# The convolution half of a two-layer kernel, rewritten as 337 pieces in one fixed order, with the transposes and the short convolution on TensorE

## The chip, the cores and the metric

One core of one Trainium2 chip. The metric is the device time of one execution in microseconds (us); smaller is better. Runs of the kernel before scatter over 1%. Engines are named as the profile names them: PE is TensorE (PEld its weight loads), DVE is VectorE, ACT is ScalarE, POOL is GpSimd, SP issues the loads and stores.

## The reference, cut to what matters

Two layers, each made of a gated long convolution (`_A_ref`) and an MLP (`_B_ref`), over 2048 tokens of 512 channels. The convolution of the first layer and that of the second have the same `k`, `v` and filter, so both kernels compute its result `y` once (in `YA`) and use it twice.

```python
def _A_ref(q, k, v, shift_k, ssm_k, ssm_D):
    # k_shift: 4-tap causal convolution of k along the tokens, per channel
    for t in range(ks):
        k_shift = k_shift + k_pad[:, t:t + S, :] * shift_k[:, ks - 1 - t][None, None, :]
    kv = k_shift * v
    # y: kv convolved with ssm_k over the whole length 2048 (by FFT of 4096), per channel
    y_f = rfft(kv padded) * rfft(ssm_k padded)
    y = irfft(y_f)[:S] + kv * ssm_D
    return q * y

def _B_ref(x, w1, b1, w2, b2):            # 512 -> 1376 -> 512
    h = gelu(layernorm(x) @ w1 + b1)
    return h @ w2 + b2

x = q
for layer in range(2):
    x = x + _A_ref(layernorm(x), k, v, shift_k, ssm_k, ssm_D)
    x = x + _B_ref(layernorm(x), w1, b1, w2, b2)
```

Both kernels do the long convolution as a transform in two stages, by matrix products with tables. A "first stage" multiplies by `Ft` over 128 partitions, a transposition brings the other index into the partitions, and a "second stage" multiplies by one table of `Wt` for each of 32 frequencies. The spectrum of `kv` (called X) is multiplied by that of the filter (called K, in `ZK`, with its swapped halves in `KSW`). The inverse goes back the same way: tables `Mt` (called V), a transposition, tables `Gt` (called Y).

## The kernel before

The short convolution and the product with `v` are on VectorE, 28 + 4 operations of 128x2048 elements on four blocks of 128 channels:

```python
    def kv_chunk(cc):                                                   # line 148
        ...
        nc.vector.tensor_tensor(m[:], kh[:, h:h + NT, c0:c0 + CW], sb(0), ALU.mult)
        for t in range(1, KS):
            m2 = rot.tile([P, NT, CW], BF16, name="kvt", tag="kvt")
            nc.vector.tensor_tensor(m2[:], kh[:, h - t:h - t + NT, c0:c0 + CW], sb(t), ALU.mult)
            nc.vector.tensor_tensor(m[:], m[:], m2[:], ALU.add)
        nc.vector.tensor_tensor(uv[:, :, c0:c0 + CW], m[:], uv[:, :, c0:c0 + CW], ALU.mult)
```

The first stage ends in a transposition on VectorE, eight times (K and `kv`, four blocks each), and so does the inverse, four times:

```python
        def stage1(src, dst, cc, tag):                                  # line 191
            ...
            for q in range(4):
                pz = ps.tile([P, 8, CW], F32, name="pz", tag=tag)
                for i in range(8):
                    tau = 8 * (q % 2) + i
                    nc.tensor.matmul(pz[:, i, :], Ft[:, q // 2, :], src[:, tau, c0:c0 + CW], start=True, stop=True)
                nc.scalar.activation(ZT[:, 8 * q:8 * q + 8, :], pz[:], AF.Copy)
            nc.vector.transpose(dst[:, :, c0:c0 + CW].bitcast(F32).rearrange("p k c -> p c k"),
                                ZT[:].bitcast(F32).rearrange("p b c -> p c b"))
        ...
        k_transpose()                                                   # line 209
        for cc in range(NCH):
            kv_chunk(cc)
            stage1(Ktok, ZK, cc, "pa")
            stage1(uv, ZX, cc, "pb")
        ...
        for j in range(NA // 2):                                        # second stage of K
            k_stage2(j)
        ...
        for j in range(NA // 2):                                        # X, product T, inverse V
            T = x_mul(j)
            if pend is not None:
                x_inv(j - 1, pend)
            pend = T
        ...
        for cc in range(NCH):                                           # line 264
            c0 = cc * CW
            nc.vector.transpose(V2[:, :, c0:c0 + CW].bitcast(F32).rearrange("p k c -> p c k"),
                                ZX[:, :, c0:c0 + CW].bitcast(F32).rearrange("p b c -> p c b"))
        for t2 in range(NT // 2):                                       # output Y
            ...
```

The second stage works on whole rows of 512 channels, so each loop over j needs every block of the loop ahead of it: all first stages before any second stage, all inverses before any inverse transposition. After that come the gate, a layernorm and the MLP: eight groups (two layers of four) of 512 tokens. `prep` (two layernorms and a gate on VectorE) of the next group is issued beside the MLP of this one.

## Time and profile before

| | before |
|---|---|
| time, median of 4 runs | 340.26 us (338.0 to 340.95) |
| span and granted clock of the profiled run | 337.7 us, 0.884 |
| busy PE / DVE / ACT | 243.3 / 225.2 / 164.5 us |
| first MLP matmul | 170.13 us |

The busy numbers hide what matters: 72%, 67% and 49% of the span are averages over stages with different limits. So the page's slices, its chain, and the table by stage are to be read together. Two words to know for them: the "front" is all up to the first MLP matmul, and the granted clock is the share of full speed that TensorE was allowed.

### The profile page before, as it was taken

How to read it: one execution, taken by the hardware profiler on the slowest of the kernel's cores; microseconds unless marked ns; L12 is line 12 of the kernel's file. 1: busy time of each engine (PE TensorE's matmuls, PEld its weight loads, DVE VectorE, ACT ScalarE, POOL GpSimd, SP SyncE). 2: the span in 40 equal slices, each digit the busy share in tenths (PEclk: the TensorE clock that was granted, in tenths of full speed). 3: DMA queues.
4: the chain of work that ended last, by engine and by line, in shares of the span. 5: the costliest groups of instructions: out<-in, count | busy, mean ns of one | idle time of the engine just before them, and what ended most of it. 6: DMA issues, size and time to landing. Idle time of an engine off the chain costs nothing.

```text
span 337.7 us, 3467 instructions
## 1 busy us (share of the span) xinstructions
PE 243.3 (72%) x1292; PEld 123.1 (36%) x1312; DVE 225.2 (67%) x361; ACT 164.5 (49%) x206; POOL 19.8 (6%) x26
## 2 busy tenths in 40 slices
PE   0007646253675987007599999989999999999995
PEld 0007646152321332002235444444444444444442
DVE  2208999999543999894887987888787682020122
ACT  0106877055779887004667736246271643826300
POOL 3000000000010000001102112101011110000000
PEclk9999767556587999656969999999999999999999
DMA  7990000006589444000000000000000001010011
GB/s 235 369 390 4 2 0 2 0 0 249 188 227 225 108 167 167 0 0 0 2 0 1 2 0 0 2 0 1 3 0 0 2 0 52 12 46 17 18 62 47
DMA packets 7040, 21.94 MB, mean 65 GB/s; under 512 B 912, under 2 KB 4593, under 8 KB 5872
## 3 DMA queue, kind: packets, MB, share of 16 engines
q1 hardware_dynamic: 5890, 19.14, 17.9%
q10 hardware_dynamic: 1022, 2.59, 2.1%
q8 instruction: 10, 0.16, 0.2%
q0 software_dynamic: 112, 0.00, 0.1%
q14 instruction: 6, 0.05, 0.0%
HBM read 15.44 MB, written 2.10 MB: 52 GB/s over the span
## 4 chain that ended last, share of the span: by engine, by line
DVE 46%; PE 36%; DMA 8%; ACT 5%; POOL 3%; issue 2%; another core or an unknown queue 0%; DVEq 0%; POOLq 0%; ACTq 0%
PE po L328 17%; PE ph L316 14%; DVE arena L200 7%; DVE st L169 6%; DMA arena<-in_A_ssm_k_dram 6%; DVE arena L266 5%; DVE kvm L159 4%; DVE kvt L158 4%; DVE arena L177 4%; ACT arena L207 3%; DVE T L235 3%; POOL rs L173 3%; DVE arena L244 3%; DVE T L234 2%; DMA arena<-in_A_k_dram 2%
## 5 line engine op out<-in xcount | busy, mean ns | idle before, releaser
L328 PE MATMUL po<-arena 128*128 128x512 bf16 (+1 forms) x339 | 79.6, 379 | 2.1 <-DVE arena L331 1.4
L316 PE MATMUL ph<-arena 128*128 128x512 bf16 (+1 forms) x349 | 79.3, 386 | 0.8 <-ACT arena L308 0.7
L318 ACT ACTIVATE arena<-ph,B 128x512 bf16<-128x512 f32 (+1 forms) x88 | 60.2, 687 | 29.4 <-PE ph L316 27.4
L331 DVE TENSOR_TENSOR arena<-po,arena 128x512 bf16<-128x512 f32 x32 | 21.8, 682 | 50.1 <-PE po L328 50.1
L316 PEld LDWEIGHTS <-arena 128*128 128x128 bf16 (+1 forms) x352 | 35.8, 102 | 43.3 <-issue 3.8
L328 PEld LDWEIGHTS <-arena 128*128 128x128 bf16 (+1 forms) x352 | 33.8, 98 | 38.9 <-issue 1.5
L198 PE MATMUL pz<-arena,Ft 128*128 128x128 bf16 x256 | 26.7, 283 | 26.4 <-DVE arena L160 17.2
L169 DVE BATCH_NORM_STATS2 st<-arena 128x6 f32<-128x512 bf16 x64 | 42.4, 676 | 4.8 <-DMA arena<-in_A_q_dram 4.1
L199 ACT ACTIVATE ZT<-pz 128x1024 bf16<-128x1024 f32 x32 | 30.7, 1031 | 22.2 <-PE pz L198 21.9
L308 ACT ACTIVATE arena<-pt 128x512 bf16<-128x512 bf16 x32 | 17.3, 594 | 42.9 <-PE pt L307 42.7
L198 PEld LDWEIGHTS <-Ft 128*128 128x128 bf16 x256 | 23.7, 132 | 29.5 <-issue 25.0
L200 DVE STREAM_TRANSPOSE arena<-ZT 128x2048 f32<-128x2048 f32 x8 | 29.4, 3676 | 3.0 <-ACT ZT L199 3.0
L173 POOL TENSOR_TENSOR rs<-rs,mhalf 128x4 f32<-128x4 f32 x16 | 16.1, 1009 | 202.4 <-DVE rs L172 202.4
L187 PE MATMUL pk<-IDt,arena 128*128 128x128 bf16 x64 | 6.3, 279 | 27.2 <-DVE arena L143 26.6
L273 PE MATMUL py<-arena,Gt 128*128 128x512 bf16 x31 | 9.5, 450 | 18.1 <-DVE arena L266 17.6
L177 DVE TENSOR_SCALAR arena<-arena,rs,nm 128x512 bf16<-128x512 bf16 x64 | 22.1, 407 | 0.6
L242 PE MATMUL pv<-T,arena 128*128 128x512 bf16 x63 | 18.3, 388 | 3.3 <-DVE T L234 1.5
L274 ACT ACTIVATE arena<-py 128x1024 bf16<-128x1024 f32 x8 | 8.2, 1023 | 21.7 <-PE py L273 21.5
L232 ACT ACTIVATE xb<-px 128x1024 bf16<-128x1024 f32 x16 | 16.3, 1040 | 3.4 <-DVE T L235 3.3
L207 ACT ACTIVATE arena<-pk 128x1024 bf16<-128x1024 f32 x16 | 15.1, 1058 | 2.6 <-PE pk L206 2.6
L189 ACT ACTIVATE arena<-pk 128x2048 bf16<-128x2048 bf16 x4 | 7.2, 1883 | 18.7 <-PE pk L187 18.7
L266 DVE STREAM_TRANSPOSE arena<-arena 128x2048 f32<-128x2048 f32 x4 | 16.2, 4149 | 0.1
(38 smaller groups left out, 188.2 us busy)
## 6 DMA issues: line engine op xcount, KB each, us to landing
arena<-arena SPq DMA_DIRECT2D x8, 512.0 KB, 7.4
arena<-in_A_k_dram SPq DMA_DIRECT2D x1, 2048.0 KB, 12.6
arena<-in_A_ssm_k_dram ACTq DMA_DIRECT2D x4, 512.0 KB, 19.4
arena<-in_A_v_dram SPq DMA_DIRECT2D x1, 2048.0 KB, 12.7
arena<-tabM SPq DMA_DIRECT2D x1, 2048.0 KB, 7.6
arena<-in_A_q_dram SPq DMA_DIRECT2D x1, 2048.0 KB, 8.7
out_dram<-arena SPq DMA_DIRECT2D x16, 128.0 KB, 1.7
arena<-in_B_w_dram SPq DMA_DIRECT2D x1, 1376.0 KB, 5.9
```

Source lines behind the costliest of these rows:

```text
L169: nc.vector.bn_stats(st[:, i, :], x_t[:, GT * g + i, :])
L173: nc.gpsimd.tensor_tensor(rs[:], rs[:], mhalf[:], ALU.pow)
L177: nc.vector.tensor_scalar(out=dst[:, i, :], in0=x_t[:, GT * g + i, :], scalar1=rs[:, i:i + 1], scalar2=nm[:, i:i + 1], op0=ALU.mult, op1=A ...
L198: nc.tensor.matmul(pz[:, i, :], Ft[:, q // 2, :], src[:, tau, c0:c0 + CW], start=True, stop=True)
L199: nc.scalar.activation(ZT[:, 8 * q:8 * q + 8, :], pz[:], AF.Copy)
L200: nc.vector.transpose(dst[:, :, c0:c0 + CW].bitcast(F32).rearrange("p k c -> p c k"), ZT[:].bitcast(F32).rearrange("p b c -> p c b"))
L207: nc.scalar.activation(ZK[:, 2 * j:2 * j + 2, :], pk[:], AF.Copy)
L266: nc.vector.transpose(V2[:, :, c0:c0 + CW].bitcast(F32).rearrange("p k c -> p c k"), ZX[:, :, c0:c0 + CW].bitcast(F32).rearrange("p b c -> ...
L316: nc.tensor.matmul(ph[0:m, :], W1t[:, ct, ft * P:ft * P + m], lt[:, ct, :], start=ct == 0, stop=ct == CT - 1)
L318: nc.scalar.activation(ht[0:m, ft, :], ph[0:m, :], AF.Gelu_apprx_tanh, bias=B1[0:m, ft:ft + 1])
L328: nc.tensor.matmul(po[:], ht[0:m, ft, i * P:(i + 1) * P], W2t[0:m, ft, :], start=ft == 0, stop=ft == FT - 1)
L331: nc.vector.tensor_tensor(xs, po[:], xs, ALU.add)
```

## The change

The intent: take from VectorE what TensorE can do (the transpositions by a matmul against the identity, the short convolution by matmuls against diagonal matrices), cut every stage but K's second to blocks of 128 channels so that blocks need not wait for each other, and fix in which order each engine does the pieces, so that loads, TensorE-heavy and VectorE-heavy stages lie beside each other. Four PSUM slots of 1024 fp32 serve all pieces of the front. The order is a string.

```diff
+ORDER = """
+lK2.S lK1.S lK3.S lH.S lv0.S lK0.S lk2.S lW.S lv1.S lG.S lk0.S lk3.S lk1.S KT2.P0 KT2e.D dt2.D K2S0.P10 KT1.P2 K2S0e.A
...
+U2S3.P2 U2S0e.A U2S2.P0 U2S1.P1 U2S2e.A U2S3e.D U1T0.P3 U2S1e.A kv30.P0 U1T0e.D X10.P20 kvm30.D X11.P11 X10e.A U1T1.P3
+X11e.A U3S0.P00 T10.D0 U1T1e.D U0T0.P2 U3S0e.A U3S2.P1 U0T0e.D X13.P32 U3S2e.A U3S1.P0 U3S3.P2 T11.D1 X13e.A U0T1.P1
...
+"""
```

A word is a piece, its engine's letter (P, D, A, G for GpSimd, S) and the slots it takes. K2S0 is the first quarter of the first stage of K's block 2, K2S0e its copy out of PSUM, kv30 a part of the convolution and kvm30 its product with `v`, U the first stage of `kv`, T after a block the transposes. X10, T10, V10 are X, product and inverse of block 1, quarter 0; TP and Y the inverse's transposes and the output. The pieces are written down with

```diff
+    def write(self, order):
+        pieces = {it["name"]: it for it in self.items}
+        for word in order.split():
+            name, how = word.split(".")
+            it = pieces.pop(name)
+            it["eng"] = how[0]
+            it["slot"] = {ring: int(c) for ring, c in zip(it["take"], how[1:])}
+            it["fn"](it)
...
+        with tc.manual_schedule(engines={ENG.PE, ENG.Activation, ENG.DVE, ENG.Pool, ENG.SP}):
+            plan.write(ORDER)
+            n2 = prep(2)
```

and the work itself moves like this (cut):

```diff
-        nc.vector.tensor_tensor(m[:], kh[:, h:h + NT, c0:c0 + CW], sb(0), ALU.mult)
-        for t in range(1, KS): ...
+                    for i in range(8):                                          # kv
+                        for t in range(KS):
+                            tau = 8 * o2 + i - t
+                            w = kT[:, cc, tau, 2:2 + P] if tau >= 0 else kT[:, cc, tau + NT, 1:1 + P]
+                            nc.tensor.matmul(o[:, i, :], w, DG[:, cc, t, :], start=t == 0, stop=t == KS - 1)
...
-            nc.vector.transpose(dst[:, :, c0:c0 + CW].bitcast(F32).rearrange("p k c -> p c k"),
-                                ZT[:].bitcast(F32).rearrange("p b c -> p c b"))
+                    for i in range(16):                                         # T of a first stage
+                        zk = apf(ZTb[z["slot"]["zt"]], 16 * h + i, [[8 * D, P], [32, P]])
+                        nc.tensor.transpose(o[:, i, :], zk, IDt[:])
...
-            nc.vector.transpose(V2[:, :, c0:c0 + CW].bitcast(F32).rearrange("p k c -> p c k"),
-                                ZX[:, :, c0:c0 + CW].bitcast(F32).rearrange("p b c -> p c b"))
+                        for i in range(2 * m):                                  # TP
+                            vk = apf(ZTb[v0["slot"]["zt"]], 16 * (i // m) + t0 + i % m, [[8 * D, P], [32, P]])
+                            nc.tensor.transpose(o[:, i // m, i % m, :], vk, IDt[:])
...
-    with tc.tile_pool(name="ps2", bufs=3, space=bass.MemoryType.PSUM) as ps2, \
-            tc.tile_pool(name="ps3", bufs=2, space=bass.MemoryType.PSUM) as ps3:
+    with tc.tile_pool(name="ps2", bufs=3, space=bass.MemoryType.PSUM, reuse_waits="tile") as ps2, \
+            tc.tile_pool(name="ps3", bufs=2, space=bass.MemoryType.PSUM, reuse_waits="tile") as ps3:
```

The preps of the MLP's first three groups move into the ordered part (those of groups 0 and 1 cut into pieces, with some on ScalarE and GpSimd). The loops of the MLP stay as they were.

## The prediction

> **What bounds the kernel now.** I read the busy digits of the page first, then its chain of work, then a table of engine busy time by stage, then the groups of instructions by shape, then single stretches of the timeline for the pitch of back-to-back work.
>
> The busy digits (40 slices of 8.44 us, tenths):
> ```profile
> PE   0007646253675987007599999989999999999995
> ...
> DVE  2208999999543999894887987888787682020122
> ACT  0106877055779887004667736246271643826300
> ...
> PEclk9999767556587999656969999999999999999999
> ```
> PE is at 8 or 9 from the twenty-second slice to the last but one (the MLP). Before that, no engine is at 9 throughout: DVE is, then ACT, then DVE, in turn, and PE runs at a half-granted clock in between. The chain of work says the same:
> ```profile
> DVE 46%; PE 36%; DMA 8%; ACT 5%; POOL 3%; issue 2%; another core or an unknown queue 0%; DVEq 0%; POOLq 0%; ACTq 0%
> ```
> By stage (start:end, length, then busy us and counts of PE, PEld, DVE, ACT, POOL; granted clock; DMA):
> ```profile
> 0.00:26.60 26.60, 0.00 (x0) 0.00 (x0) 4.66 (x8) 1.28 (x1) 2.69 (x8) 1.00 0.87 317
> 26.60:92.30 65.70, 36.30 (x327) 30.60 (x329) 62.61 (x38) 41.31 (x40) 0.00 (x0) 0.67 0.15 53
> 92.30:107.10 14.80, 9.50 (x28) 3.10 (x28) 4.55 (x15) 12.42 (x15) 1.04 (x1) 0.85 0.94 238
> 107.10:137.50 30.40, 24.94 (x90) 8.29 (x92) 28.58 (x41) 22.60 (x23) 0.00 (x0) 0.95 0.50 141
> 137.50:153.70 16.20, 0.00 (x0) 0.00 (x0) 16.19 (x4) 0.00 (x0) 0.00 (x0) 0.50 0.00 0
> 153.70:170.10 16.40, 11.34 (x47) 4.83 (x48) 9.97 (x27) 10.36 (x13) 3.00 (x4) 0.81 0.00 1
> 170.10:337.70 167.60, 161.22 (x800) 76.27 (x815) 98.62 (x232) 76.57 (x117) 13.08 (x13) 0.99 0.04 13
> ```
> So there are two kernels in one. The front (170.1 us, up to the first MLP matmul) is a row of stages, each bound by another thing: 26.6 us of loads, 65.7 us of VectorE, 14.8 us of ScalarE, 30.4 us of VectorE, 16.2 us of VectorE alone, 16.4 us of a latency chain. The MLP (167.6 us) is TensorE at full clock: 704 matmuls of 512 columns at a pitch of 0.216 us are 152 us, the rest is transposes and ends. The change touches only the front in substance.
>
> The operations at stake (busy us, mean ns):
> ```profile
> L200 DVE STREAM_TRANSPOSE arena<-ZT 128x2048 f32<-128x2048 f32 x8 | 29.4, 3676 | 3.0 <-ACT ZT L199 3.0
> L266 DVE STREAM_TRANSPOSE arena<-arena 128x2048 f32<-128x2048 f32 x4 | 16.2, 4149 | 0.1
> L159 DVE TENSOR_TENSOR kvm<-kvm,kvt 128x2048 bf16<-128x2048 bf16 x12 | 14.4, 1210 | 0.1
> L158 DVE TENSOR_TENSOR kvt<-arena,SK 128x2048 bf16<-128x2048 bf16 x12 | 14.2, 1215 | 0.0
> L199 ACT ACTIVATE ZT<-pz 128x1024 bf16<-128x1024 f32 x32 | 30.7, 1031 | 22.2 <-PE pz L198 21.9
> L189 ACT ACTIVATE arena<-pk 128x2048 bf16<-128x2048 bf16 x4 | 7.2, 1883 | 18.7 <-PE pk L187 18.7
> ```
> and two timeline lines for the pitch:
> ```profile
> 43.05 0.61 PE L198 MATMUL pz<-arena,Ft 128*128 128x128 bf16 x8 [0.31 <-ACT ZT L199]
> 95.95 10.19 ACT L207 ACTIVATE arena<-pk 128x1024 bf16<-128x1024 f32 x11 [0.68 <-PE pk L206]
> ```
> Eight 128-column matmuls take 0.61 us, one alone 0.22: pitch (0.61-0.22)/7 = 56 ns. Eleven evictions take 10.19 us: pitch 0.926 us, not 1.03. A VectorE bf16 product starts every 1.14 us in a row of them.
>
> **What the Trainium skill says.** (1) "Perfetto Trace Analysis", Optimization Strategy: where the most contended engine changes over time, interleave those regimes. The stage table is such a case. (2) "TensorE: Matmul & The Clock Gate", Back-to-back issue gap: pairs of weight load and matmul sustain some 81 ns at 128 columns, and 56 ns is for the isolated gap. The short bursts here show 56 ns with a weight load each, so I use 56; long bursts at full clock are not in this trace. (3) The same page, HAM oscillation: idle gaps take the clock down. The trace agrees: 0.67 granted in the gappy second stage, 0.99 in the MLP. (4) "VectorE: DVE Perf Modes", The perf-mode tier table: a copy out of PSUM is at most 2x, a two-tensor op with PSUM 1x. The 1.22 us fp32 casts of 1024 elements (line L244) agree with 1x; a VectorE copy of 2048 bf16 out of PSUM is not in this trace, and 2x would make it about 1.2 us.
>
> **The change part by part.** The front is rewritten as 337 pieces in a fixed order on five queues, with four PSUM slots of 1024 fp32.
> Removed from VectorE: 12 stream transposes, 45.6 us; the shift convolution, 12+12+4 products and sums and 4 products with v, 39 us; together 85 of its 127 us of front work (the DVE column summed over the first six stages).
> Added to TensorE: the transposes (128 for K, 128 for U, 128 for the inverse, 64 of k), the convolution as 256 matmuls against diagonal matrices, and the X, inverse and output products cut to 128 columns. Count after, with the MLP's first 16 transposes: 528 transposes and 768 matmuls of 128 columns at 56 ns = 72.6 us; 128 of 256 columns at 112 ns (estimate, twice 56) = 14.3; 32 of 512 at 216 ns = 6.9. Sum 94 us at full clock, against some 53 before by the same pitches.
> VectorE after, from the letters in the order, at 1.1 to 1.14 us a piece: 16 products T 18.2; 8 products with v out of PSUM 9.1; 18 fp32 evictions 19.8; 20.5 bf16 evictions of 2048 (estimate 1.14) 23.4; diagonals, layernorm and gates 18. Sum 89 us.
> ScalarE after: 70 fp32 evictions at 0.926 = 65; 11.5 bf16 ones at 1.79 (the 1.883 less the same overlap) = 20.6; one layernorm and two MLP transposes 4.5. Sum 90 us.
> So the front goes from one engine at a time to three engines at about 90 us each. A floor is: first load of 512 KB (estimate 5 us: the load of SKr, the same size, took 6.2 from issue beside other traffic), 94 us of TensorE, and the part of the tail where TensorE waits (last inverse, eviction, transposes, output, gate, layernorm, about 11 us of which TensorE works half): 105 us. Three in-order engines at 90 us each with four slots cannot all be full. I walked the order by hand with these durations, 0.2 us for each hand-over between engines (the 0.18 that ACT waits after PE in the timeline), and a piece starting when its engine, inputs and slot are free. Milestones: K first stage done at 36 us, K second stage at 51, first product T at 68, last product T at 108, last inverse at 112, first MLP matmul at 126. Loads stay hidden in that walk: the swapped halves are issued at 52.6 and land by 61 (8.5 us before), q is issued at 92.5 and needed at 103, the MLP weights are issued at 108 and needed at 126.
> MLP: same 704 matmuls, same pitch, one cold start as before (the first 44 took 11.9 instead of 9.7 us); the 1.4 us that TensorE waited near 221 us for VectorE may go. I take 166 to 168, no gain.
> Sum: 126 + 166 = 292 us of span, plus 2 us (the profiled run reported 339.74 for a span of 337.7): 294. That is 13.5% less.
>
> **The rivals.** (a) TensorE cannot hold 56 ns when every 128-column matmul has a new, often strided, weight: at the 81 ns of the skill 1296 of them cost 32 us more, TensorE becomes the only bound and the total is about 320. For: the strided transposes L187 average 279 ns against 224 for L307. Against: those fell partly in a half clock, and L307, with a new weight each, shows 55 ns. (b) The clock stays half in gaps of the piecewise front, as in 26.6 to 92.3: 20 us more, 314. Against: my walk has TensorE 80% busy, denser than the stage at 107 to 137 that was granted 0.95. (c) VectorE copies bf16 PSUM at 1x, 2.2 us: 20.5 pieces cost 21 us more on VectorE, and about 15 in the time: 309. (d) The hand-overs are shorter than I took and the order is as dense as its maker hoped: front 116, total 284. (e) Slower than before: only if an undetected wait serialises stages again; the front would have to lose 44 us.
>
> **Range and chances.** (a), (b) and (c) together a fifth, mostly in part; (d) a fifth. So 284 to 306 eight times in ten. Faster by over 2% 0.96, within 2% 0.02, slower 0.02.
>
> **What would show it.** In the profile after: no stream transposes and some 2,270 matmuls; the first MLP matmul near 126 us; in the front PE, DVE and ACT each busy 70 to 80% at once; a granted clock of 0.9 or more from 15 us on; DVE bf16 PSUM copies at 1.2 us; 128-column bursts of 16 at 56 to 60 ns; an MLP of 166 to 168 us. A first MLP matmul after 140 would make the prediction wrong, and so would an MLP that is longer because prep of the second and third group comes late.

## The result, and the profile after

| | before | after |
|---|---|---|
| time, median | 340.39 us (16 runs, 338.0 to 341.36) | 291.37 us (10 runs, 291.19 to 293.8) |
| ratio | | 0.8577, 95% interval 0.8554 to 0.8599 |
| profiled run: span, clock | 337.7 us, 0.884 | 289.5 us, 0.994 |
| busy PE / DVE / ACT | 243.3 / 225.2 / 164.5 us | 264.2 / 188.6 / 171.2 us |
| first MLP matmul | 170.13 us | 124.63 us |
| from there to the end of the span | 167.6 us | 164.9 us |

A ratio here and below is the mean time of one kernel's fast runs over that of the other's of the same rounds, so it is not quite the ratio of the medians that are quoted. The kernel is 14% faster, 2.6 us below the predicted 294.

The same rows of the page, 40 slices, now of 7.24 us:

```profile
PE   2698999999789999589998999999999999999994
...
DVE  0387976669499999897888787886867720110221
ACT  1288867657998999888735806626427337157000
...
PEclk9999999999999999799999999999999999999999
```

TensorE reaches 9 in the third slice and is below 7 only once from there to the last but one (the seventeenth slice, where the front ends); in slices 12 to 16 all three engines stand at 8 or 9 at once, as before in two slices of the front only (14 and 15). The clock row has one 7; that it shows 9 at the start is not to be trusted (see below). The chain of work of the page turned with it, from VectorE to TensorE:

```profile
PE 64%; DVE 21%; ACT 5%; DMA 3%; issue 2%; POOL 2%; ACTq 0%; DVEq 0%
```

The table by stretch (start:end, length, then busy us and counts of PE, PEld, DVE, ACT, POOL; granted clock; DMA share; GB/s). The first four lines are the front, cut where the work changes; the last is the MLP:

```profile
0.00:38.00 38.00, 28.74 (x342) 25.63 (x344) 23.41 (x37) 23.38 (x20) 3.12 (x12) 1.00 0.64 233
38.00:66.00 28.00, 27.12 (x354) 22.77 (x354) 19.18 (x16) 17.79 (x19) 0.00 (x0) 1.00 0.75 182
66.00:97.00 31.00, 27.22 (x433) 25.83 (x432) 25.65 (x23) 28.04 (x29) 0.52 (x1) 1.00 0.19 70
97.00:124.60 27.60, 22.07 (x334) 21.28 (x333) 25.82 (x63) 25.23 (x26) 5.86 (x9) 0.94 0.30 104
124.60:289.50 164.90, 159.01 (x800) 75.78 (x815) 94.53 (x229) 76.75 (x117) 17.54 (x28) 1.00 0.04 14
```

From 38 to 66 us TensorE is busy 97% of the time and is the bound. From 66 to 97 three engines are at 83 to 90%. From 97 on VectorE and ScalarE are at 91 to 94%. Nothing like the stretch before with VectorE alone is left.

The groups at stake, by shape (busy us, mean ns, idle time of the engine ahead and what ended it):

```profile
L210 DVE COPY arena<-p 128x2048 bf16<-128x2048 bf16 x20 | 24.1, 1219 | 13.6 <-PE p L343 11.7 <-ACT ZT L208 0.6 <-PE p L375 0.5
L428 DVE TENSOR_TENSOR T<-xb,arena 128x2048 bf16<-128x2048 bf16 x16 | 19.3, 1219 | 5.2 <-PE p L440 4.9 <-ACT xb L208 0.2
L321 PE MATMUL p<-IDt,ZT 128*128 128x128 bf16 x256 | 18.7, 227 | 0.0
L321 PEld LDWEIGHTS <-ZT 128*128 128x128 bf16 x256 | 17.9, 150 | 0.1
L440 PE MATMUL p<-arena,T 128*128 128x128 bf16 x256 | 16.6, 219 | 3.2 <-ACT arena L208 2.0 <-DVE ZT L210 0.7 <-DVE T L428 0.3
L391 PE MATMUL p<-DG,arena 128*128 128x128 bf16 x256 | 15.6, 219 | 0.1
L391 PEld LDWEIGHTS <-arena 128*128 128x128 bf16 x256 | 14.9, 98 | 1.3 <-issue 0.2
L397 DVE TENSOR_TENSOR arena<-p,arena 128x1024 bf16<-128x1024 f32 x8 | 9.8, 1225 | 6.8 <-PE p L391 5.1 <-ACT arena L208 1.4 <-issue 0.3
```

The first line is the copy that the prediction had to guess: 2048 bf16 elements out of PSUM in 1.219 us. The convolution that cost VectorE 39 us is now 15.6 us of TensorE (L391) and 9.8 us of products with `v` (L397). No stream transpose appears on the page.

Two bursts of the timeline of PE (start, length, then the group) give the pitch:

```profile
22.53 1.18 PE L321 MATMUL p<-IDt,ZT 128*128 128x128 bf16 x16
...
46.38 1.95 PE L391 MATMUL p<-DG,arena 128*128 128x128 bf16 x32
```

One matmul alone takes 0.22 us (their means, 219 to 227 ns). So the convolution's pitch is (1.95 - 0.22)/31 = 56 ns, and that of the transposes (1.18 - 0.22)/15 = 64 ns. The transposes' weights are read with a stride of 32 elements, and their weight loads take 150 ns where the convolution's packed ones take 98.

At the start, the timeline of PE shows something that the prediction lacks:

```profile
4.73 1.92 PE L343 MATMUL p<-IDt,arena 128*128 128x128 bf16 x16 [4.73 <-DMA arena<-in_A_ssm_k_dram]
9.88 1.01 PE L305 MATMUL p<-Ft,arena 128*128 128x256 bf16 x4 [3.22 <-DMA Ft<-tabF]
10.68 1.91 PE L343 MATMUL p<-IDt,arena 128*128 128x128 bf16 x16
...
20.21 1.15 PE L343 MATMUL p<-IDt,arena 128*128 128x128 bf16 x16
```

TensorE has its first transposes done at 6.65 us and then waits 3.22 us for the table `Ft`. That load is 64 KB, is issued third on ScalarE's queue, and took 8.1 us from issue to landing. Ahead of it on the same queue is a 4 KB load of the taps (`sT`) in pieces of 8 bytes, which took 7.6.

The lines show a second thing. The same 16 transposes take 1.92 and 1.91 us at first and 1.15 us at 20.21 us: pitches of 113 and 62 ns. So up to about 14 us TensorE ran at about half its later pace, though the granted clock of that stretch is given as 1.00. It is given as 1.00 too for the first 26.6 us of the kernel before, in which no matmul ran at all; so at the start of these traces the record of the clock says nothing, and the pitch has to be read.

The first burst of the MLP and a later wait of TensorE, before:

```profile
170.13 11.86 PE L316 MATMUL ph<-arena 128*128 128x512 bf16 x43 [0.69 <-ACT arena L308]
...
221.73 0.59 PE L328 MATMUL po<-arena 128*128 128x512 bf16 x2 [1.41 <-DVE arena L331]
```

and the first burst after:

```profile
124.63 9.66 PE L581 MATMUL ph<-arena 128*128 128x512 bf16 x43 [1.35 <-ACT arena L208]
```

Before, the first burst took 2.2 us longer: it began at a lowered clock, behind 32 us in which TensorE was first silent and then busy only in parts (0.50 and 0.81 granted). After, there is no such start. The wait of 1.41 us for VectorE's additions, which stand in its queue behind the preps, has become one of 0.88 us (at 153.29).

### The profile page after: what moved, and what is told of

It is laid out like the page before. It is cut to its first block, busy times and chain, and to the rows that moved or that the text cites. A ratio compares the mean times of both kernels' runs of the same rounds, so it can differ in the third digit from the quotient of the medians.

```text
span 289.5 us, 5469 instructions
## 1 busy us (share of the span) xinstructions
PE 264.2 (91%) x2253; PEld 171.3 (59%) x2272; DVE 188.6 (65%) x365; ACT 171.2 (59%) x207; POOL 27.0 (9%) x50
## 4 chain that ended last, share of the span: by engine, by line
PE 64%; DVE 21%; ACT 5%; DMA 3%; issue 2%; POOL 2%; ACTq 0%; DVEq 0%
PE po L593 23%; PE ph L581 20%; DVE lst L226 6%; PE p L391 5%; PE p L321 4%; DVE arena L210 3%; DMA Ft<-tabF 3%; DVE T L428 3%; PE p L305 2%; PE p L440 2%; POOL lrs L235 2%; DVE arena L244 2%; ACT arena L208 2%; PE pt L572 2%; DVE ZT L210 2%
## 5 line engine op out<-in xcount | busy, mean ns | idle before, releaser
L208 ACT ACTIVATE arena<-p 128x1024 bf16<-128x1024 f32 (+3 forms) x34 | 41.8, 1278 | 9.0 <-PE p L391 2.3
L208 ACT ACTIVATE ZT<-p 128x1024 bf16<-128x1024 f32 x36 | 36.0, 1034 | 15.8 <-PE p L305 14.8
L226 DVE BATCH_NORM_STATS2 lst<-arena 128x6 f32<-128x512 bf16 (+2 forms) x68 | 41.5, 651 | 0.7
L210 DVE COPY arena<-p 128x2048 bf16<-128x2048 bf16 (+1 forms) x21 | 24.7, 1193 | 13.6 <-PE p L343 11.7
L244 DVE TENSOR_SCALAR arena<-arena,lrs,lnm 128x512 bf16<-128x512 bf16 x60 | 21.1, 408 | 15.8 <-POOL lnm L236 15.8
L235 POOL TENSOR_TENSOR lrs<-lrs,mhalf 128x4 f32<-128x4 f32 (+1 forms) x18 | 18.4, 1023 | 105.9 <-DVE lnm L232 105.9
L305 PE MATMUL p<-Ft,arena 128*128 128x256 bf16 x128 | 18.6, 281 | 4.8 <-DMA Ft<-tabF 3.2
L428 DVE TENSOR_TENSOR T<-xb,arena 128x2048 bf16<-128x2048 bf16 x16 | 19.3, 1219 | 5.2 <-PE p L440 4.9
L440 PE MATMUL p<-arena,T 128*128 128x128 bf16 x256 | 16.6, 219 | 3.2 <-ACT arena L208 2.0
L321 PE MATMUL p<-IDt,ZT 128*128 128x128 bf16 x256 | 18.7, 227 | 0.0
L321 PEld LDWEIGHTS <-ZT 128*128 128x128 bf16 x256 | 17.9, 150 | 0.1
```

What stands on the lines that cost most here:

```text
L208: nc.scalar.activation(dst, src, AF.Copy)
L210: nc.vector.tensor_copy(dst, src)
L226: nc.vector.bn_stats(self.st[:, i, h, :], x_t[:, GT * g + i, c0:c9])
L235: nc.gpsimd.tensor_tensor(self.rs[:, a:b], self.rs[:, a:b], mhalf[:, a:b], ALU.pow)
L244: nc.vector.tensor_scalar(out=dst[:, i, :], in0=xs, scalar1=sc, scalar2=bi, op0=ALU.mult, op1=ALU.add)
L305: nc.tensor.matmul(o[:, i, :], src[:, 4 * q + i, cs], Ft[:].rearrange("p x m -> p (x m)"), start=True, stop=True)
```

## The experiments

The theory, A: the gain is the front's, and it comes from both parts together. VectorE lost 85 us of work, and the order puts what is left side by side; under this order the three engines are so full that any work given back comes back in the time. The rivals: B, moving the work alone is enough, the order adds little (or the other way round: the order alone is enough and there is slack for the moved work); and others for single terms, the clock, the waits of the PSUM pools, the start of the MLP. Ten kernels ran. Differences in us are of medians, to the 291.37 us of the kernel after where nothing else is said; taken from the ratios they come out within 1 us of these.

### 1. The same pieces, in order of stages

All 337 pieces, their engines and tiles as after. Only the order (and with it the slots) is changed: stage by stage, each piece followed by its copy, with one piece of lookahead (cut to one line of each order):

```diff
-U1T1.P3 X11e.A U3S0.P00 T10.D0 U1T1e.D U0T0.P2 U3S0e.A U3S2.P1 U0T0e.D X13.P32 U3S2e.A U3S1.P0 U3S3.P2 T11.D1 X13e.A
+X00.P00 X00e.A T00.D0 X01.P11 X01e.A T01.D1 V00.P22 V00e.D X02.P32 X02e.A T02.D2 V01.P0 V01e.A X03.P10 X03e.A T03.D0
```

> The changed kernel's 337 pieces, the same engine for each, but in the order of the stages (K first stage, K second stage, k transposed, convolution and U, X/T/V, outputs), each with one piece of lookahead on TensorE; slots dealt round. Theory A (the gain needs the interleaving of the stages as well as the moved work): the stages are bound by different engines again, estimate by summing them 5+31+12+4+32+30+10+18 = 142 us to the first MLP matmul instead of 124.6, so about 308 us in all (300 to 320). Rival B (moving the work off VectorE is all, the order is worth little): 291 to 296 us.

Measured: 324.85 us (324.42 to 325.05, 4 runs), ratio 0.9536 (0.9501 to 0.957), correct. The first MLP matmul is at 157.94 us, the clock 0.974. A slice of 10 us, first of this kernel (one of the two in which VectorE is emptiest):

```profile
100.00:110.00 10.00, 6.74 (x112) 6.05 (x109) 4.62 (x4) 8.78 (x10) 0.00 (x0) 1.00 0.01 2
```

and then a slice of the kernel after in the corresponding work:

```profile
90.00:100.00 10.00, 9.71 (x167) 9.54 (x165) 9.50 (x9) 9.38 (x10) 1.04 (x2) 1.00 0.01 2
```

The same work on the same engines, but in order of stages each engine is busy some two thirds of the time (PE 6.6, DVE 6.6 and ACT 6.8 of 10 us on the mean from 80 to 160 us), since X, its copy, the product, the inverse and its copy go round from engine to engine and few rounds are in flight. The groups of this kernel say it in their last columns (busy, mean ns, idle ahead):

```profile
L208 ACT ACTIVATE ZT<-p 128x1024 bf16<-128x1024 f32 x36 | 35.5, 1024 | 35.9 <-PE p L305 30.2 <-PE p L440 5.7
L428 DVE TENSOR_TENSOR T<-xb,arena 128x2048 bf16<-128x2048 bf16 x16 | 19.5, 1224 | 13.8 <-ACT xb L208 13.7
L440 PE MATMUL p<-arena,T 128*128 128x128 bf16 x256 | 17.8, 225 | 11.7 <-DVE T L428 11.7
```

The product waits 13.8 us where it waited 5.2, the inverse 11.7 where it waited 3.2, at the same mean durations. What follows: of the 49 us, the moved work with the cut into blocks gives 15.5 us in this plain order, and the interleaved order 33.5 more. Rival B falls. I had expected 308 (300 to 320), so the order was worth about twice what I thought. The miss lies at the end: the last transposes of the first stages start at 85.2 us, where my sum of stages had 84, but from there to the first MLP matmul it took some 73 us for the 58 summed. The kernel after starts its last such transposes at 88.0 us, no earlier; but by then it has done 9 of the 16 products and 6 of the 16 groups of inverse matmuls, and this one has just begun. How much a better order of stages with more lookahead would recover was not tried.

### 2. The inverse's transpositions back on VectorE

```diff
-    INV = "PPPP"
+    INV = "DDDD"
```

with the TP pieces of the order replaced by four stream transposes, at the place of each block's first TP copy.

> The inverse transform's four transposes go back from TensorE to VectorE (4 stream transposes of about 4.15 us, 16.6 us, in place of 9 TensorE groups and their evictions on ACT and DVE). Theory A (VectorE has no room left in the late front, 9.3 to 9.9 of 10 us busy from 80 to 110 us): the net 12 us on VectorE show as 8 to 14 us, 300 to 305 us in all. Rival B (VectorE is only 65% busy over the whole, so it absorbs them): under 4 us, below 295.

Measured: 307.61 us (306.4 to 308.29, 4 runs), ratio 0.9032 (0.8985 to 0.908). The result was wrong (relative error 0.0247), and the edited order shows why: the word Y28, the second half of block 2's output, stands before TI2, the stream transpose that it needs. The trace has it so:

```profile
114.21 1.06 PE L461 MATMUL p<-arena,Gt 128*128 128x128 bf16 x16
...
116.80 4.17 DVE L469 STREAM_TRANSPOSE arena<-arena 128x2048 f32<-128x2048 f32 x1
```

Those 16 matmuls read what the filter's spectrum had left in that place. (Worked out in floating point from the reference's formulas with random inputs of its sizes, not run on the chip, this one slip gives an error of 0.025 to 0.028.) So one wait is missing from this run, a wait that could only have held TensorE back; I use the time, but a corrected order was not run. The stretch where the first transposes lie:

```profile
100.00:110.00 10.00, 2.71 (x25) 2.54 (x25) 9.96 (x7) 0.59 (x1) 0.00 (x0) 0.50 0.00 0
```

Four transposes of 4.16 us are 16.6 us on VectorE. Its busy time over the whole run rises only 12.4 us (201.0 for 188.6), as copies fall away, and ACT has less to do (163.2 for 171.2); still the time rises by 16.2 us. A stream transpose needs all four inverses of its block, so in this order TensorE has little to do while it runs: 2.7 of 10 us, at half clock. So A holds, and the loss is more than VectorE's own added work and above the 8 to 14 us expected.

### 3. The convolution's load given back to VectorE

28 extra products of 128x2048 bf16, on scratch, ahead of the products with `v`. The result stays right, TensorE keeps its convolution.

```diff
                     us = uv[:, 8 * o2:8 * o2 + 8, cs]
+                    dgf = DG[:].rearrange("p a b c -> p (a b c)")
+                    for _ in range(4 - o2):
+                        nc.vector.tensor_tensor(at(145 * K, [[1, 2048]]), dgf, dgf, ALU.mult)
                     nc.vector.tensor_tensor(us, view(pf[pe["slot"]["ps"]], [8, P]), us, ALU.mult)
```

> The changed kernel plus 28 VectorE products of 128x2048 bf16 on scratch data, 3 or 4 before each product with v: the VectorE load that the convolution had before (28 of its 32 instructions), about 32 us at a pitch of 1.14. TensorE still does its 256 matmuls. Theory A: VectorE is busy about 20 of the 28 us in which the convolution runs, so some 8 us are absorbed and 20 to 26 show: 311 to 318 us. Rival B (VectorE's 35 us of slack in the front absorb nearly all): under 8 us, below 299.

Measured: 320.26 us (319.79 to 320.72, 4 runs), ratio 0.9403 (0.9368 to 0.9437), correct. The group added, and a slice of 10 us in that stretch:

```profile
L399 DVE TENSOR_TENSOR arena<-DG 128x2048 bf16<-128x2048 bf16 x28 | 34.2, 1221 | 0.7
```

```profile
50.00:60.00 10.00, 7.32 (x68) 5.59 (x68) 9.83 (x10) 3.88 (x4) 0.00 (x0) 0.82 0.36 79
```

Of 34.2 us added (32 at the pitch of 1.14), 28.9 come back in the time. The slack of VectorE in this stretch (about a third of it is idle after) hides only some 3 to 5 us, where I had expected some 8: VectorE becomes the bound and TensorE behind it drops to 0.82 of its clock. This is not the old code, only its load; it says that with this order the convolution's load on VectorE would cost some 29 us. What the move as a whole is worth it does not say, since TensorE still does its 256 matmuls here. The 29 us and the 33.5 us of experiment 1 cannot be added: each part is worth much because the other is there.

### 4. Half the convolution's matmuls

```diff
-                        for t in range(KS):
+                        for t in range(2):
...
-                            nc.tensor.matmul(o[:, i, :], w, DG[:, cc, t, :], start=t == 0, stop=t == KS - 1)
+                            nc.tensor.matmul(o[:, i, :], w, DG[:, cc, t, :], start=t == 0, stop=t == 1)
```

This leaves out two taps. The comparison with the reference still passes: the convolution's part of the output is too small for its tolerance. (By the same reckoning as in experiment 2, leaving the whole convolution out changes the output by about 0.013%.) So here only the time is of use, and "correct" in the other experiments says little about the convolution's arithmetic.

> Wrong result on purpose: the convolution with two of its four taps, 128 matmuls of 128 columns fewer (7.2 us of TensorE at 56 ns), same evictions. Theory A (TensorE, 92 to 98% busy between 10 and 70 us, is what bounds that stretch): 5 to 7 us less, 284.5 to 286.5 us. Rival B (the evictions and the slots bound it, TensorE's busy share is latency): 0 to 2 us less.

Measured: 286.05 us (285.6 to 286.25, 4 runs), ratio 0.8397 (0.8366 to 0.8427). 128 matmuls fewer are 7.2 us at 56 ns; 5.3 of these come off the time, and the first MLP matmul is at 119.44 instead of 124.63. So TensorE sets the pace in that stretch, as the 97% of the table by stretch said.

### 5. The kernel after once more, and 6. the table `Ft` loaded first

Run with experiments 7 and 8. Number 5 is the kernel after unchanged, as the yardstick for differences of 1 us. Number 6 swaps two loads:

```diff
     nc.scalar.dma_start(IDt[:], ident_h.ap().bitcast(BF16))
-    nc.scalar.dma_start(sT[:], A_shift_k.rearrange("(ct p) k -> p ct k", p=P))
     nc.scalar.dma_start(Ft[:], F_h.ap().bitcast(BF16))
+    nc.scalar.dma_start(sT[:], A_shift_k.rearrange("(ct p) k -> p ct k", p=P))
```

> The changed kernel once more, as the base of the two small edits beside it: 291 to 292 us, first 44 MLP matmuls at full pitch (9.7 us).

> The table of the first stage (64 KB) is asked for before the small shift weights (4 KB in pieces of 8 bytes) instead of after them. TensorE waited 3.2 us for it, to 9.88 us. If the small pieces hold it up, it lands about 2 to 3 us earlier, the first first-stage matmul starts at about 8.2 us (when VectorE is done with the first eviction) and, TensorE being busy from then on, 1 to 1.7 us of that reach the end: 289.7 to 290.5. Rival: it shares the DMA engines with the 1.5 MB of K in front of it and lands no earlier, 0 us; or the gain is taken up by a later wait, 0 us.

Measured: after again 291.57 us (291.12 to 292.54, 5 runs), ratio 0.8569 (0.8539 to 0.86); with `Ft` first 289.96 us (289.45 to 290.71, 5 runs), ratio 0.8521 (0.849 to 0.8551), correct, as expected. The intervals of the two ratios overlap because the kernel before scatters; of the runs themselves, every one with `Ft` first is below every one without. The second line of PE's timeline is now

```profile
8.18 1.04 PE L305 MATMUL p<-Ft,arena 128*128 128x256 bf16 x4 [1.57 <-DVE arena L345]
```

It starts 1.70 us earlier, and what it waits for is no more a load: the table landed 4.4 us after its issue. The first MLP matmul is 1.64 us earlier (122.99) and the time 1.6 us shorter. (The two starts are against the profile of the kernel after; against that of number 5 they are 1.55 and 1.48 us.) So the wait for the table was on the path to the end, in full as far as it could be removed, and this is the fastest version that leaves nothing out.

### 7. One more move in the order

In addition to 6, the second group's layernorm on ScalarE (s12) goes from ahead of the first group's last copies to a place shortly behind them, because VectorE's gates were waiting for those copies.

```diff
-Y08.P1 Y18e.A TP30.P0 ga.D Y08e.A TP34.P2 TP38.P3 s12.A TP30e.D gs.D Y30.P1 Y30e.A TP38e.A gl2.D gl0.D gp02.G TP34e.A
-Y38.P0 gp00.G gb02.D Y34.P1 Y38e.A LT02.P3 gb00.D Y34e.A LT02e.A h2.D LT00.P2 LT00e.A h0.D hs2.D hs0.D gp12.G gb12.D
+Y08.P1 Y18e.A TP30.P0 ga.D Y08e.A TP34.P2 TP38.P3 TP30e.D gs.D Y30.P1 Y30e.A TP38e.A gl2.D gl0.D gp02.G TP34e.A Y38.P0
+gp00.G gb02.D Y34.P1 Y38e.A LT02.P3 gb00.D Y34e.A s12.A LT02e.A h2.D LT00.P2 LT00e.A h0.D hs2.D hs0.D gp12.G gb12.D
```

> The former edit, and the layernorm of the second group on ScalarE (2.93 us) moved from before to after the last output evictions. In the changed kernel TensorE waits 3.4 us for ScalarE near 119 us and VectorE 0.4 us near 117. If that wait sets the start of the MLP, up to 1 us more than the former; if VectorE's statistics and gates set it (they run to 122.6 with one gap of 0.4), under 0.5 us; if the second group then comes late, 0 or a loss.

Measured: 294.2 us (293.93 to 296.27, 6 runs), ratio 0.865 (0.8618 to 0.8681), 4.2 us slower than 6. The first burst of the MLP:

```profile
124.03 11.86 PE L581 MATMUL ph<-arena 128*128 128x512 bf16 x44 [3.10 <-ACT arena L208]
```

The gates do start earlier. But s12, 2.9 us long, now sits ahead of the copies of the MLP's first transposes (LT02e, LT00e) on ScalarE's queue: TensorE waits 3.10 us for them where it waited 1.11 in number 6, and the burst starts 1.04 us later and then runs in part at a lowered clock, 11.86 for 9.66 us. The second group comes late as well: its gates start at 122.19 us for 121.03, and TensorE's later wait for VectorE grows from 1.03 to 2.23 us. The three add up to the loss: 1.0, 2.2 and 1.2 us. My placement was poor. A place behind LT00e was not tried. It also shows how narrow the order is: one piece, started 6.7 us later (119.23 for 112.55), cost more than swapping the loads gave.

### 8. The kernel before with a warm start of the MLP

56 idle transposes ahead of the first group's real ones:

```diff
                 pt = ps3.tile([P, CT, P], BF16, name="pt", tag="pt")
+                if n == 0 and i == 0:
+                    for d in range(56):
+                        nc.tensor.transpose(pt[:, d % CT, :], IDt[:], IDt[:])
```

> The kernel before with 56 dummy transposes of the identity just before the first MLP transposes, where TensorE waits 3.5 us. Tests the term that the prediction had wrong (the MLP takes 2.7 us less after the change). Theory: 2.2 us of it are the half clock at the MLP's start, so the first 44 matmuls take 9.7 instead of 11.9 us and the whole about 2 us less than before (338). Rival: VectorE's layernorms, in the chain up to 221 us, hold the MLP back, and the whole does not move.

Measured: 339.68 us (338.0 to 341.06, 6 runs), ratio 0.9972 (0.9932 to 1.0012). The interval reaches from 2.3 us less to 0.4 us more, so by the time alone it settles neither for the 2 us expected nor for the rival; the trace says more. The clock was mended:

```profile
172.08 9.66 PE L319 MATMUL ph<-arena 128*128 128x512 bf16 x44 [0.69 <-ACT arena L311]
...
201.72 0.59 PE L331 MATMUL po<-arena 128*128 128x512 bf16 x2 [1.87 <-DVE arena L334]
...
223.03 0.59 PE L331 MATMUL po<-arena 128*128 128x512 bf16 x2 [1.24 <-DVE arena L334]
```

but now TensorE waits for VectorE twice, 3.11 us in all, where the kernel before waited 1.41. That takes back 1.7 of the 2.2 us, and the idle transposes themselves, which end at 169.4, held up the real ones by about 1 us (VectorE had their input 1.2 us later than in the kernel before, they started 2.2 us later). From the first group's start to the fourth's it is 53.8 us, for 54.4 before and 51.7 after. So a warm start alone, made in this way, gives nothing that shows above the scatter: VectorE's preps are the next bound. After, those of the first groups are already on their way in the front.

### 9. The PSUM pools' waits by tile, and 10. a warm second stage, both in the kernel before

Number 9 sets `reuse_waits="tile"` on the two pools of the MLP, as the change does. Number 10 puts 100 idle matmuls into each block of the stage at 26.6 to 92.3 us:

```diff
                 pz = ps.tile([P, 8, CW], F32, name="pz", tag=tag)
+                if q == 0 and src is uv:
+                    for i in range(100):
+                        nc.tensor.matmul(pz[:, i % 8, :], IDt[:], IDt[:], start=True, stop=True)
```

> The kernel before with only the change's new option on the two PSUM pools of the MLP (wait per tile when a buffer is reused). Theory: no part of the gain, within 1 us of before. Rival: it lets the MLP start earlier, 1 to 3 us.

> The kernel before with 100 dummy matmuls of 128 columns in each of the four column blocks of the second stage (26.6 to 92.3 us), in TensorE's waits, so that its clock is granted there. Theory A: VectorE, busy 62.6 of 65.7 us, bounds that stage, so a clock near 1 instead of 0.67 moves the time by under 2 us either way. Rival C (a good part of the gain is the clock): 5 us or more less.

Measured: number 9, 341.06 us (339.92 to 341.55, 4 runs), ratio 1.0005 (0.9948 to 1.0063): no part of the gain. Number 10, 343.32 us (341.94 to 344.21, 4 runs), ratio 1.0079 (1.0025 to 1.0133). Its stage:

```profile
26.60:92.30 65.70, 46.24 (x631) 42.47 (x632) 59.60 (x39) 37.58 (x37) 0.00 (x0) 0.84 0.11 36
```

The granted clock there rose from 0.67 to 0.84 and the time did not fall; it rose by some 2.5 us, a little more than the 2 us either way that were expected, as the idle matmuls (some 300 of the 400 fall into this stretch) held up real ones (the last stream transpose of the stage begins at 92.22 instead of 88.63). So a better clock, bought in this way, gave nothing in that stage, where VectorE is the bound; how much the idle matmuls cost for themselves was not separated.

## Why the prediction was right, step by step

**The bound.** The step "the front is a row of stages, each bound by another thing" and the sums of removed work (85 us of VectorE) hold: experiment 3 gave 34 us of it back and got 29 in the time, experiment 2 gave 16.6 back (12.4 net) and got 16.2. Two readings on the way were off, without weight in the sum: the pitch of ScalarE's evictions divides 10.19 us by eleven, and by the method used for the matmuls it is 0.917 us, not 0.926; and the walk at 80% is not denser than the stage at 107 to 137 us, where TensorE's busy column has 24.94 of 30.4 us, 82%.

**Durations.** The bf16 copy out of PSUM took 1.219 us on VectorE (taken: 1.14 at the pitch, 1.2 for one), within the 2x that the Trainium skill, "VectorE: DVE Perf Modes", The perf-mode tier table, allows a copy out of PSUM, so rival (c) falls. The pitch of 128-column matmuls with a new packed weight each is 56 ns in bursts of 32, so rival (a), 81 ns, falls. The term for strided weights was under-sized: 64 ns, and with 448 such transposes (64 for K, 256 behind the first stages, 128 behind the inverse) this is 448 x 8 ns = 3.6 us of TensorE. The record of the clock gives 0.994 over the run, above the 0.9 asked for from 15 us on, so rival (b), 20 us, falls. But it is not free of slow stretches: the bursts up to 14 us ran at about half pace (113 ns), and so did part of those at 119 to 123 us, behind a wait of 3.37 us (24 matmuls in 2.49 us, for 1.52 in number 7).

**Sums and the walk.** In the front PE, DVE and ACT were busy 105, 94 and 94 us (the sums of the first four stretches) against 94, 89 and 90. TensorE's busy time contains the end of each burst and so is more than a sum of pitches: the 32 bursts of 256 columns, 14.3 us at the pitch, show 18.6. The strided weights are another 3.6. The remaining 3 us are about what the slow bursts cost besides: the three groups of transposes before 14 us 1.8 (1.92, 1.91 and 1.37 us, for 1.15 later), the 24 output matmuls and 16 transposes at 119 to 123 us 1.7 (2.49 and 1.74 us, for 1.52 and 1.06). Milestones of the walk:

| | predicted | measured |
|---|---|---|
| K first stage done | 36 us | about 35 |
| K second stage done | 51 us | about 51 |
| first product T starts | 68 us | 66.3 |
| last product T done | 108 us | 106.1 |
| last inverse done | 112 us | 109.9 |
| first MLP matmul | 126 us | 124.6 |

So the walk was 1.4 to 2.1 us late from T on, in spite of the start that it had too early: its floor lets TensorE run from 5 us, and it missed the 3.22 us wait for `Ft`, worth 1.6 us at the end (experiment 6). The step "loads stay hidden in that walk" failed in that one load. The others stayed hidden. The swapped halves were issued by 53.3 us (52.6 predicted) and the MLP weights at 106 to 108 (108). For q the walk was far off, 92.5 for 70.5, without effect. The closeness is in part luck: the strided weights, the slow bursts and the wait for `Ft` are up to some 8 us of TensorE and waiting that the walk did not have, and it must have taken other waits too long by as much. Which ones is not known, since only its milestones are on record.

**The MLP.** "One cold start as before ... 166 to 168, no gain" was the mis-sized term: it took 164.9 us. The missing cold start is 2.2 us of the difference (9.66 for 11.86) and the shorter wait for VectorE (0.88 for 1.41) the other 0.5. Experiment 8 shows that in the kernel before the first alone gives nothing above the scatter; that it needs the preps brought forward is what its longer waits for VectorE say, and was not tested by itself. In experiment 1, which has the same pieces for the preps in another order, the MLP took 164.9 us too. So these 2.7 us come from the rewritten end of the front and not from the interleaving.

**Rival (d)**, hand-overs shorter and a front of 116 us, was not reached; the measured front lies between the walk and it.

**What the prediction did not say.** It did not split the gain between order and moved work. Experiment 1 does, and my guess there (308) was off by 17 us: in a plain order the engines wait for each other far more than I had reckoned. Why exactly 33.5, how far more lookahead in a plain order would go, and what experiment 2 takes with its order put right stay open.

## What to carry to other kernels

When a profile shows one engine after another at 9 and the rest waiting, add up each engine's work over the whole region and aim for the largest sum: moving work to the idle engine and interleaving the stages belong together, and the first alone gave here a third of what both gave. When engines are balanced in this way, most of any added work comes back (28.9 of 34.2 us in experiment 3), so measure small things (a table queued behind a load of tiny pieces, one layernorm in the wrong place in a queue) at their place in the order. A clock that is low while another engine is the bound was not worth mending with idle matmuls here. And in a fixed order a piece can stand before the one that it needs (experiment 2): check the order against the data flow, not only the output against a tolerance.

## What the Trainium skill lacked or had wrong

- "TensorE: Matmul & The Clock Gate", Back-to-back issue gap, gives some 81 ns for sustained pairs of weight load and matmul at 128 columns and 131 ns at 512. Here 32 such pairs with packed weights ran at 56 ns, and the MLP's 512-column matmuls at 0.216 us; the page's isolated figures (56 and 216) fit sustained bursts.
- The same section gives no figure for strided weights. "SBUF — State Buffer", Door 1: The DMA port swizzle, says that a stride beyond 8 bf16 elements has a price, without saying it of weight loads. Here a stride of 32 elements made a weight load 150 instead of 98 ns and the pitch 64 instead of 56 ns; that the one causes the other is inferred, as no run changed the stride alone.
- "Perfetto Trace Analysis", Optimization Strategy, advises to interleave regimes and gives no size. Here the same pieces in order of stages took 324.85 us and interleaved 291.57.
- No page that I read gives a figure for what a load of tiny pieces costs one queued behind it: here 64 KB behind 4 KB in pieces of 8 bytes landed after 8.1 us, and after 4.4 us when put ahead; its first user started 1.70 us earlier.
